# Two of the first tile's output blocks by seven products, and a new order of work around it

## The chip, the cores and the metric

One core of one Trainium2 chip. The metric is the device time of one launch in microseconds, as the median of several executions. Below, TensorE is PE in the profile (its weight loads PEld), VectorE is DVE, ScalarE is ACT, GpSimd is POOL, and SP is the engine whose queue issues nearly all DMAs.

## The reference

A recurrent attention with decay, and behind it a bilinear feed-forward layer (four sequences of 768 tokens, 8 heads of 64; model width 512, hidden width 1536):

```python
for t in range(S):
    state = gamma * state + einsum('bhd,bhde', k[t], v[t])   # per head, outer product
    y[t] = scale * einsum('bhd,bhde->bhe', q[t], state)
x = y reshaped to [3072, 512]
out = ((x @ w_a) * (x @ w_b)) @ w_out                         # float32
```

## The kernel before

The 3072 tokens are 24 slots of 128, taken in pairs. The attention of a slot is done in chunk form: k and q are scaled by powers of the decay and cast to bf16 (`scaled`, L239, mostly on POOL), k and q are transposed, `scores` (L273) gives the products of keys and queries, DVE masks them (L279), `update` (L290) adds to the state in a PSUM bank, and `inter` (L310) and `intra` (L320) give y, which ACT copies out as x, the feed-forward's input. `turn(new, old)` brings in pair `new` (state and scores) and finishes pair `old` (y's). Pairs 0 to 2 (slots 0 to 5) come by a variant with transposes on TensorE (`flip2`, L375; `update2`, L404; `inter2`, L416; `intra2`, L427); from slot 6 on the transposes are DMAs (L254).

The feed-forward works in tiles of 4, 2, 2, 2, 2, 4 and 8 slots (`TILES`). In a tile, hidden block `ft` (128 of the 1536 hidden columns) is two chains of four matmuls: `ffn_a` (L462), copied out by ACT, and `ffn_g` (L472), multiplied by it on DVE into `ht` (L474). `blocks(J, a, b)` does hidden blocks a to b of tile J. These chains rotate through three PSUM banks, the pool `psff`.

The output of a tile is by output blocks of 128 tokens. Tile 0's four are plain: `ffn_out` (L493), 12 matmuls of 512 columns each. The other tiles take two output blocks together as a 2x2 block product by seven products for eight (`Group`, with p1 to p7 of six matmuls of 256 columns, L561). They need sums of weights (`weight_sums`) and of h (`hsum`, s = 1 to 4, L503: on DVE in tile 1, on POOL in tiles 2 to 4). The products that share bank A follow one another in it: ACT takes a snapshot between them (L568), and DVE adds the snapshot to what leaves bank B or C. p6 reads sum 2, p7 sum 3, p5 sum 1, p3 sum 4. `single(J, ...)` runs tile J's group between the first three hidden blocks of tile J + 1. The last tile has its hidden blocks by seven products as well (`Unit`), with sums of w_a and w_b on POOL (`weight_pieces`).

The order on each engine is the order of the calls, written out by hand (`seq` chains the instructions of an engine in program order). A wait at the head of an engine's queue holds all that stands behind it. `casts(t)` puts on POOL slot t's k, q and (but for slots 12 to 19, whose v is cast by ACT in `v_cast`) v, and on SP's queue the transpose of slot t and behind it the loads of slot t + 2 (`load_slot`; the load of q is for two slots). The weights come in six parts of each matrix, each loaded in float32 (`load_w`, `load_o`, in the order of `LOADS`) and cast by POOL (`cast_w`, `cast_o`, L206). `warm` (L448) issues products of zeros into a bank.

Of the kernel before, what the change touches and what calls it, by code (L numbers as in the profile page):

```python
# [19 lines left out]
LOADS = "p0 p1 w0 w1 w2 w3 w4 k2 q2 a5 v2 b5 o0 o1 o2 o3 o4 o5 s6 s7".split()  # L20
# [3 lines left out]
def kernel(  # L24
# [39 lines left out]
    psff = ctx.enter_context(tc.tile_pool(name="psff", bufs=3, space=bass.MemoryType.PSUM))  # L64
    psat = ctx.enter_context(tc.tile_pool(name="psat", bufs=1, space=bass.MemoryType.PSUM))
    psst = ctx.enter_context(tc.tile_pool(name="psst", bufs=1, space=bass.MemoryType.PSUM))


# [14 lines left out]
    def load_slot(t):  # L83
        b, ci = divmod(t, NCH)
        for nm, src in (("k", k), ("q", q), ("v", v)):
# [8 lines left out]
            seq(nc.sync.dma_start(out=raws[nm, t], in_=s))  # L94

# [28 lines left out]
    def issue_loads(n):  # L124
        for _ in range(min(n, len(pending))):
            what = pending.pop(0)
            n = int(what[1:])
            if what[0] in "ab":
                load_w(n, what[0])
            elif what[0] in "kqv":  # L130
                load_two(what[0], {"k": k, "q": q, "v": v}[what[0]], 0, n, 2 * n)
            else:
                {"p": load_pair, "s": load_slot, "w": load_w, "o": load_o}[what[0]](n)
# [74 lines left out]
    def cast_w(j, names="ab"):  # L208
        sl = slice(j * WC, (j + 1) * WC)
        for nm, dst in (("a", wa_bf), ("b", wb_bf)):  # L210
            if nm in names:
                cast(nc.gpsimd, dst[:, :, sl], wst[nm, j])
# [33 lines left out]
    def casts(t):  # L246
        new_nat(t)
        scaled(nc.gpsimd, t, 0)
        scaled(nc.gpsimd, t, 1)
        if t not in range(12, 20):  # L250
            cast(nc.gpsimd, vb[t], raws["v", t])
        if t % 2 == 0:
            kqT[t // 2] = tra.tile([P, 2, 2, HP, P], BF16, tag="kqT", name="kqT", bufs=3)
        seq(nc.sync.dma_start_transpose(  # L254
            out=kqT[t // 2][:, t % 2].rearrange("p a b c -> p (a b) c"),
            in_=kqb[t].rearrange("p a hp r d -> p (a hp r d)")))
        if t + 2 < NSLOT:
            load_slot(t + 2)
# [9 lines left out]
    def scores(t, where):  # L268
        at = score_banks(where)
        for hp in range(HP):  # L270
            for c in range(2):
                for r in range(2):
                    seq(nc.tensor.matmul(at[r][half(c), hp, :],  # L273
                                         kqT[t // 2][half(r), t % 2, 0, hp, half(c)],
                                         kqT[t // 2][half(r), :, 1, hp, half(t % 2)],
                                         start=True, stop=True, skip_group_check=True))
        aT[t] = tra.tile([P, 2, HP, P], BF16, tag="aT", name="aT")
        for r in range(2):
            seq(nc.vector.tensor_tensor(aT[t][:, r], at[r], mask.to_broadcast([P, HP, P]), op=ALU.mult))  # L279

# [87 lines left out]
    def flip2(u, i, on, pool=psff, tag="ff"):  # L368
        if i == 0:
            kqT2[u] = tra.tile([P, 2, 2, HP, P], BF16, tag="kqT2", name="kqT2", bufs=2)  # L370
        for pars, eng in on:
            tp = pool.tile([P, 2, HP, P], BF16, tag=tag, name="tp")[:, : len(pars)]
            for n, par in enumerate(pars):
                for hp in range(HP):
                    seq(nc.tensor.transpose(tp[:, n, hp, :], kqb[2 * u + par][:, i, hp, :, :], ident))  # L375
            cast(eng, kqT2[u][:, pars[0] : pars[0] + len(pars), i], tp)

    def scores2(u, par, where="at"):
# [10 lines left out]
        for r in range(2):  # L389
            seq(nc.vector.tensor_tensor(aT[t][:, r], at[r], masks[par].to_broadcast([P, HP, P]),  # L390
                                        op=ALU.mult))

# [52 lines left out]
    def warm(pool, tag, *cols):  # L445
        idle = pool.tile([P, HP * P], F32, tag=tag, name="idle")
        for n in cols:
            seq(nc.tensor.matmul(idle[:, :n], zero[:, :P], zero[:, :n], start=True, stop=True,  # L448
                                 skip_group_check=True))

# [4 lines left out]
    def ffn_a(J, ft, c0=0, c1=None):  # L455
# [4 lines left out]
        a = psff.tile([P, 4 * P], F32, tag="ff", name="a")[:, : c1 - c0]  # L460
# [4 lines left out]
        seq(nc.scalar.copy(asb, a))  # L465

    def ffn_g(J, ft, c0=0, c1=None):
        c1 = TILES[J] * P if c1 is None else c1
        fs = slice(ft * P, (ft + 1) * P)
        g = psff.tile([P, 4 * P], F32, tag="ff", name="g")[:, : c1 - c0]  # L470
        for kt in range(KT):
            seq(nc.tensor.matmul(g, wb_bf[:, kt, fs], xcols(J, kt, c0, c1),  # L472
                                 start=(kt == 0), stop=(kt == KT - 1)))
        seq(nc.vector.tensor_tensor(ht[J][:, ft, c0:c1], g, asbs.pop((J, ft, c0)), op=ALU.mult))  # L474

# [12 lines left out]
    def ffn_out(J, i):  # L488
        store()
        osb = osbp.tile([P, DM], F32, tag="osb", name="osb")  # L490
        o = psff.tile([P, DM], F32, tag="ff", name="o")
        for ft in range(NFT):
            seq(nc.tensor.matmul(o, ht[J][:, ft, i * P : (i + 1) * P], wo_bf[:, ft],  # L493
                                 start=(ft == 0), stop=(ft == NFT - 1)))
        cast(nc.scalar, osb, o)
        held.append((rows(J, i // 2, i % 2), osb))
# [10 lines left out]
    def weight_sums(a, b):  # L507
        if not T1:
            T1.append(wstage.tile([P, NP, DH], BF16, tag="w", name="wsum1"))
        j = slice(a, b)  # L510
        tt(T3[:, j], B22[:, j], B12[:, j], ALU.subtract)
        tt(T2[:, j], T3[:, j], B11[:, j], ALU.add)
        tt(T4[:, j], B21[:, j], T2[:, j], ALU.subtract)
        tt(T1[0][:, j], B12[:, j], B11[:, j], ALU.subtract)

    hs = {}

    def hsum(J, s, a, b, eng=nc.vector):
        U = 2 if isinstance(J, tuple) else TILES[J] // 2
        if (J, s) not in hs:  # L520
            pool, tag = (raw, ("kf", "qf", "vf", "kf")[s - 1]) if J == (BIG, 1) else (wstage, "w")
            hs[J, s] = pool.tile([P, NP, 2, P], BF16, tag=tag, name=f"hs{s}")
        v = ht[J].rearrange("p (k j) (u r n) -> p r k j u n", k=2, r=2, n=P)
        A11, A12, A21, A22 = (v[:, r, k2, a:b, :U] for r in range(2) for k2 in range(2))
        S = {x: hs[J, x][:, a:b, :U] for x in (1, 2, 3, 4) if (J, x) in hs}
# [15 lines left out]
    class Group:  # L541

        def __init__(self, J, i, A, B, C, snaps="kqT2"):
            self.J, self.i, self.tags, self.spare = J, i, {"A": A, "B": B, "C": C}, snaps
            self.key, self.n = (J, i) if J < BIG else ((J, i // 2), i % 2)
            self.bank = {}
            self.osb = {}

        def product(self, bank, left, right, first):
            if first:  # L550
                pool, tag = self.tags[bank]
                self.bank[bank] = pool.tile([P, 4 * P], F32, tag=tag, name="m" + bank)[:, :DH]
# [33 lines left out]
        def p2(self):  # L586
            self.product("C", (0, 1), B21, True)
            tt(self.row(0)[:, :DH], self.bank["C"], self.snaps[:, 0], ALU.add)
            if self.J == BIG and self.i == 3:
# [16 lines left out]
        def p3(self):  # L606
# [8 lines left out]
            seq(nc.scalar.copy(self.row(0)[:, DH:], self.bank["A"]))  # L615
            self.leave(0)

        def p4(self):
            self.product("B", (1, 1), T4, False)
            tt(self.row(1)[:, :DH], self.bank["B"], self.snaps[:, 1], ALU.add)  # L620
            self.leave(1, 0, DH if self.J == BIG and self.i > 1 else DM)
# [57 lines left out]
    class Unit:  # L679
# [57 lines left out]
        def p3(self):  # L737
# [5 lines left out]
            else:  # L743
                tt(h_big(1)[:, self.p], self.bank["A"], half_a.pop(key), ALU.mult)

# [4 lines left out]
    def plain(w, i, c, bank):  # L750
# [10 lines left out]
        else:  # L761
            tt(h_big(c)[:, f], m, half_a.pop((i, c)), ALU.mult)

# [76 lines left out]
    ffn_a(0, 0, W2, 2 * W2)  # L840
    ffn_a(0, 1, W2, 2 * W2)
    ffn_g(0, 0, 0, W2)
# [3 lines left out]
    for ft in range(2, NFT):  # L846
# [7 lines left out]
        if ft == 7:  # L854
            scaled(D_, 4, Q)
            scaled(D_, 5, Q)
# [13 lines left out]
    ffn_g(0, 10)  # L870
# [10 lines left out]

    def v_cast(t):
        cast(nc.scalar, vb[t], raws["v", t])

    def outs(J, *rows):
        for i in rows:
            ffn_out(J, i)
# [24 lines left out]
    blocks(2, 7, 9)  # L912
    hsums(2, 0, 3, G_)
    casts(12)
    blocks(2, 9, 10)
# [20 lines left out]
    casts(16)  # L936
# [7 lines left out]
    hsum(4, 3, 0, 6, G_)  # L944
    blocks(4, 6, 8)
# [3 lines left out]
    casts(18)  # L949
# [4 lines left out]
    blocks(4, 11, NFT)  # L954
    hsums(4, 3, 6, G_)
    casts(19)
    single(4, Y0, AT0, FF)
    casts(20)
    v_cast(18)
# [3 lines left out]
    blocks(5, 5, 6)  # L963
    turn(18, 16)
# [4 lines left out]
    weight_pieces(1)  # L969
# [37 lines left out]
```

## Time and profile before

| | |
|---|---|
| median of 3 runs | 222.51 us (222.37 to 222.65) |
| the profiled execution | 222.53 us, of which the span is 220.8 us |
| PE busy in the span | 214.2 us (97%) |
| POOL busy | 140.6 us (64%) |
| DVE busy | 135.8 us (61%) |
| ACT busy | 99.2 us (45%) |

In a row of a timeline stand: start, duration, engine, line, operation, what is written and read, its shape and the number of instructions; in brackets the idle time of the engine before it and what ended that. Matmuls overlap, and the end of one is modelled: the distance of starts tells the pace. In a table of DMA issues the last number is the time from issue to landing in us.

### The profile page before, as it was taken

The numbers are of one execution on the slowest core, as the hardware profiler recorded it, in microseconds if no ns is written. First come the engines' busy times: TensorE is split into PE (matmuls) and PEld (weight loads), VectorE is DVE, ScalarE is ACT, GpSimd is POOL, SyncE is SP. The second block draws the span as 40 slices with busy tenths as digits, with TensorE's granted clock in tenths as the row PEclk, the third lists the DMA queues.
The fourth block names the chain that finished last, engine by engine and source line by source line (L and its number), as shares of the span: only waits on it lengthen the run. The fifth ranks groups of instructions, "written<-read, shape, count | busy, mean of one in ns | idle before, by whom it ended". The sixth has DMA issues, their size and how long they took to land.

```text
span 220.8 us, 5622 instructions
## 1 busy us (share of the span) xinstructions
PE 214.2 (97%) x2233; PEld 144.6 (66%) x2244; DVE 135.8 (61%) x254; ACT 99.2 (45%) x217; POOL 140.6 (64%) x155
## 2 busy tenths in 40 slices
PE   7999999999999999999999999999999999999994
PEld 3567445587458878878888665456865444448883
DVE  3785347745774473566476345776465777789642
ACT  3364333443224444354576344555536656542331
POOL 5364666777554469659846944599999999820000
PEclk9999999999999999999999999999999999999999
DMA  6999999997999999999998599990022000000055
GB/s 170 290 324 348 350 309 342 385 262 164 217 186 286 214 239 240 237 180 274 188 224 219 118 245 194 225 174 3 3 85 105 0 1 3 0 1 4 24 190 166
DMA packets 87194, 39.68 MB, mean 180 GB/s; under 512 B 57472, under 2 KB 82944, under 8 KB 87168
## 3 DMA queue, kind: packets, MB, share of 16 engines
q1 hardware_dynamic: 87024, 39.26, 76.9%
q8 instruction: 17, 0.28, 0.5%
q14 instruction: 9, 0.07, 0.1%
q10 hardware_dynamic: 144, 0.07, 0.1%
HBM read 28.31 MB, written 6.29 MB: 157 GB/s over the span
## 4 chain that ended last, share of the span: by engine, by line
PE 93%; DMA 2%; DVE 2%; issue 1%; ACT 0%; SPq 0%; DVEq 0%; ACTq 0%
PE a L462 19%; PE g L472 19%; PE mA L561 12%; PE uA L698 8%; PE mB L561 6%; PE o L493 5%; PE uB L698 4%; PE mC L561 3%; DMA qf<-in_q_dram 2%; PE at L273 2%; PE y L320 2%; PE uC L698 2%; PE st L290 2%; PE kb L756 2%; PE ka L756 2%; PE y L427 1%
## 5 line engine op out<-in xcount | busy, mean ns | idle before, releaser
L474 DVE TENSOR_TENSOR ht<-g,asb 128x256 bf16<-128x256 f32 (+1 forms) x74 | 37.1, 503 | 40.4 <-PE g L472 34.0
L472 PE MATMUL g<-xt,wb_bf 128*128 128x256 bf16 (+1 forms) x296 | 53.2, 304 | 0.4 <-DVE ht L474 0.4
L462 PE MATMUL a<-xt,wa_bf 128*128 128x256 bf16 (+1 forms) x292 | 53.4, 304 | 0.2
L465 ACT CAST asb<-a 128x256 bf16<-128x256 f32 (+1 forms) x74 | 32.2, 437 | 44.6 <-PE a L462 42.0
L472 PEld LDWEIGHTS <-wb_bf 128*128 128x128 bf16 x296 | 28.8, 98 | 13.4 <-issue 0.7
L239 POOL TENSOR_TENSOR kqb<-kf,ktab 128x512 bf16<-128x512 f32 x22 | 23.2, 1057 | 20.4 <-DMA kf<-in_k_dram 17.3
L462 PEld LDWEIGHTS <-wa_bf 128*128 128x128 bf16 x296 | 27.9, 98 | 12.2 <-issue 0.8
L561 PEld LDWEIGHTS <-hs 128*128 128x128 bf16 x240 | 23.4, 98 | 3.9
L279 DVE TENSOR_TENSOR aT<-at,mask 128x512 bf16<-128x512 f32 x36 | 22.3, 683 | 0.3
L704 ACT COPY snap<-uA 128x512 f32<-128x512 f32 x30 | 16.7, 588 | 12.6 <-PE uA L698 12.0
L239 POOL TENSOR_TENSOR kqb<-qf,qtab 128x512 bf16<-128x512 f32 x18 | 19.2, 1066 | 4.7 <-DMA qf<-in_q_dram 4.7
L503 POOL TENSOR_TENSOR hs<-ht,hs 128x384 bf16<-128x384 bf16 (+1 forms) x17 | 16.6, 982 | 5.8 <-DVE ht L474 5.8
L568 ACT COPY snaps<-mA 128x256 f32<-128x256 f32 x30 | 11.2, 373 | 19.8 <-PE mA L561 19.7
L561 PEld LDWEIGHTS <-ht 128*128 128x128 bf16 x180 | 17.5, 98 | 2.8
L503 POOL TENSOR_TENSOR hs<-ht 128x384 bf16<-128x384 bf16 (+2 forms) x12 | 13.8, 1152 | 3.7 <-DVE ht L474 3.7
L561 PE MATMUL mA<-wsum,hs 128*128 128x256 bf16 x120 | 15.7, 273 | 0.0
L206 POOL CAST vb<-vf 128x512 bf16<-128x512 f32 x16 | 10.1, 643 | 7.3 <-DMA vf<-in_v_dram 7.1
L503 POOL TENSOR_TENSOR ht<-gsb,asb 128x512 bf16<-128x512 bf16 x12 | 13.9, 1169 | 1.3 <-DVE gsb L503 1.3
L503 DVE TENSOR_TENSOR osb<-mB,snaps 128x256 f32<-128x256 f32 x20 | 8.4, 422 | 9.4 <-PE mB L561 5.1
L493 PE MATMUL o<-wo_bf,ht 128*128 128x512 bf16 x46 | 10.6, 380 | 0.1
L331 ACT CAST xt<-y 128x512 bf16<-128x512 f32 x18 | 9.7, 588 | 1.5 <-PE y L320 1.4
L448 PE MATMUL idle<-zero 128*128 128x256 f32 (+2 forms) x16 | 8.2, 632 | 1.6 <-DVE zero L140 1.5
(104 smaller groups left out, 323.0 us busy)
## 6 DMA issues: line engine op xcount, KB each, us to landing
qf<-in_q_dram SPq DMA_DIRECT2D x12, 512.0 KB, 5.7
out_dram<-osb SPq DMA_DIRECT2D x21, 256.0 KB, 3.9
kf<-in_k_dram SPq DMA_DIRECT2D x18, 256.0 KB, 4.6
vf<-in_v_dram SPq DMA_DIRECT2D x18, 256.0 KB, 5.4
wsta<-in_moe_w_a_dram SPq DMA_DIRECT2D x6, 512.0 KB, 8.4
wstb<-in_moe_w_b_dram SPq DMA_DIRECT2D x6, 512.0 KB, 8.1
wsto<-in_moe_w_out_dram SPq DMA_DIRECT2D x6, 512.0 KB, 7.6
kf<-in_k_dram SPq DMA_DIRECT2D x3, 512.0 KB, 7.1
```

The source lines that it names most:

```text
L239: seq(eng.tensor_tensor(dst, src, tab, op=ALU.mult))
L279: seq(nc.vector.tensor_tensor(aT[t][:, r], at[r], mask.to_broadcast([P, HP, P]), op=ALU.mult))
L462: seq(nc.tensor.matmul(a, wa_bf[:, kt, fs], xcols(J, kt, c0, c1), start=(kt == 0), stop=(kt == KT - 1)))
L465: seq(nc.scalar.copy(asb, a))
L472: seq(nc.tensor.matmul(g, wb_bf[:, kt, fs], xcols(J, kt, c0, c1), start=(kt == 0), stop=(kt == KT - 1)))
L474: seq(nc.vector.tensor_tensor(ht[J][:, ft, c0:c1], g, asbs.pop((J, ft, c0)), op=ALU.mult))
L493: seq(nc.tensor.matmul(o, ht[J][:, ft, i * P : (i + 1) * P], wo_bf[:, ft], start=(ft == 0), stop=(ft == NFT - 1)))
L503: seq(eng.tensor_tensor(dst, x, y, op=op))
L561: seq(nc.tensor.matmul(m, w, right[:, j], start=(first and j == 0), stop=(j == NP - 1), skip_group_check=True))
L568: seq(nc.scalar.copy(self.snaps[:, n], self.bank["A"]))
L698: seq(nc.tensor.matmul(m, w, right[:, k], start=(first and k == 0), stop=(k == 1), skip_group_check=True))
L704: seq(nc.scalar.copy(self.snaps[n], self.bank["A"]))
```

## The change

1. Tile 0: output blocks 2 and 3 go by a `Group` in place of two plain ones, spread between the halves of plain block 1 and the two turns. The sums of h that this needs (eight pieces of 128x384, on DVE) stand behind the hidden blocks 5 and 6 of tile 0 and 0 to 5 of tile 1, in buffers of the early loads. The weight sums are split into single calls. Bank reuse in `psff` is written out (class `Ring`), as some tiles are held longer.
2. The start: two of tile 0's first a's go ahead of pair 1's y's, in place of a warm-up burst, and the first two parts of each weight are cast in halves.
3. Third pair: q's scaling on DVE goes behind hidden block 8; the g's of hidden blocks 9 and 10 go ahead.
4. `casts_two(6)` casts k and q of slots 6 and 7 with their transposes ahead of both v's; loads of slots 6 to 9 go k, q, k, v, v.
5. Behind `turn(8, None)` and `turn(10, None)` three hidden blocks go as three a's, then three g's.
6. `casts` of slots 15, 16, 18 and 19 go ahead of the sums of h beside which they stood, and 8 of the last tile's 24 weight pieces go early where 1 did.

```diff
+    def casts_two(t):
+        for u in (t, t + 1):
+            new_nat(u); scaled(nc.gpsimd, u, 0); scaled(nc.gpsimd, u, 1); flip(u)
+        for u in (t, t + 1):
+            cast(nc.gpsimd, vb[u], raws["v", u])
+        load_slots(t + 2)                 # k q, k of t + 3, v, v
...
-    cast_w(0)
+    cast_w(0, parts=2)
-    warm(psff, "ff", 256)
+    ffn_a(0, 0, 0, W2)
+    ffn_a(0, 1, 0, W2)
     intra2(1, 0, True)
     inter2(1)
-    ffn_a(0, 0, 0, W2)
     intra2(1, 1, False)
     leave2(1, (A_, D_))
-    ffn_a(0, 1, 0, W2)
+    update2(1, 1)
+    ffn_g(0, 0, 0, W2)
     issue_loads(100)
-    cast_w(1)
-    update2(1, 1)
+    cast_w(1, parts=2)
...
     ffn_a(0, 9)
+    ffn_g(0, 9)
     flip2(2, Q, [((0, 1), D_)], psat, "y0")
-    ffn_g(0, 9)
+    ffn_a(0, 10)
     scores2(2, 0, "y")
     scores2(2, 1)
-    ffn_a(0, 10)
+    ffn_a(0, 11)
     update2(2, 0)
-    ffn_a(0, 11)
+    ffn_g(0, 10)
     intra2(2, 0, True)
     inter2(2)
     intra2(2, 1, False)
     leave2(2, (A_, D_))
-    ffn_g(0, 10)
     ffn_g(0, 11)
...
+    def three(J, ft):
+        store()
+        for f in range(ft, ft + 3):
+            ffn_a(J, f)
+        for f in range(ft, ft + 3):
+            ffn_g(J, f)
...
-    casts(6)
-    blocks(1, 0, 3)
-    casts(7)
-    blocks(1, 3, NFT)
-    outs(0, 0)
-    weight_sums(0, 3)
-    weight_sums(3, 6)
-    outs(0, 1)
-    casts(8)
-    outs(0, 2)
-    turn(6, None, V_)
-    hsum(1, 3, 0, 6)
-    hsums(1, 0, 6, V_)
-    outs(0, 3)
-    casts(9)
-    turn(None, 6)
+    casts_two(6)
+    for ft in range(NFT):
+        ffn_ab(1, ft)
+        if ft < 6:
+            hsum(0, (2, 1, 4)[ft // 2], ft % 2 * 3, ft % 2 * 3 + 3)
+    g = Group(0, 1, FF, FF, FF)
+    weight_sum(3)
+    weight_sum(2)
+    ffn_out(0, 0, 0)
+    ffn_out(0, 0, 1)
+    weight_sum(1, (0,))
+    casts(8)
+    g.p1()
+    g.p2()
+    weight_sum(1, (1,))
+    ffn_out(0, 1, 0)
+    turn(6, None)
+    weight_sum(4)
+    g.p7()
+    hsum(1, 3, 0, 6)
+    g.p6()
+    ffn_out(0, 1, 1)
+    g.p5()
+    casts(9)
+    turn(None, 6)
+    g.p3()
+    g.p4()
+    hsums(1, 0, 6, V_)
     single(1, AT0, AT1, FF)
...
     turn(8, None)
-    blocks(2, 7, 9)
+    three(2, 7)
...
     turn(10, None, V_)
-    blocks(3, 4, 6)
+    three(3, 4)
     hsum(3, 3, 0, 6, G_)
     v_cast(12)
-    blocks(3, 6, 8)
+    blocks(3, 7, 8)
     v_cast(13)
     blocks(3, 8, 9)
+    casts(15)
     hsums(3, 0, 3, G_)
-    casts(15)
     blocks(3, 9, 10)
     turn(12, 10)
     blocks(3, 10, NFT)
+    casts(16)
     hsums(3, 3, 6, G_)
-    casts(16)
     single(3, Y0, AT0, FF)
...
     blocks(5, 5, 6)
+    weight_pieces(6)
     turn(18, 16)
...
-    weight_pieces(1)
+    weight_pieces(2)
     turn(20, 18)
```

More of the change, by code (lines that the diff above doesn't have):

```diff
@@ L63, with __init__, tile, back @@
     osbp = ctx.enter_context(tc.tile_pool(name="osbp", bufs=6))
-    psff = ctx.enter_context(tc.tile_pool(name="psff", bufs=3, space=bass.MemoryType.PSUM))
+    ffpool = ctx.enter_context(tc.tile_pool(name="psff", bufs=1, space=bass.MemoryType.PSUM))
     psat = ctx.enter_context(tc.tile_pool(name="psat", bufs=1, space=bass.MemoryType.PSUM))
     psst = ctx.enter_context(tc.tile_pool(name="psst", bufs=1, space=bass.MemoryType.PSUM))
+    class Ring:
+        def __init__(self):
+            self.idle, self.out = ["ff0", "ff1", "ff2"], []
+        def tile(self, shape, dtype, tag, name):
+            tag = self.idle.pop(0)
+            t = ffpool.tile(shape, dtype, tag=tag, name=name)
+            self.out.append((t, tag))
+            return t
+        def back(self, *tiles):
+            for t in tiles:
+                for n, (x, tag) in enumerate(self.out):
+                    if x is t:
+                        self.idle.append(tag)
+                        del self.out[n]
+                        break
+    psff = Ring()
     last = {}
@@ L376, in flip2 @@
             cast(eng, kqT2[u][:, pars[0] : pars[0] + len(pars), i], tp)
+            psff.back(bank)
     def scores2(u, par, where="at"):
@@ L391, in scores2 @@
                                         op=ALU.mult))
+        psff.back(*at)
     def update2(u, c):
@@ L449, in warm @@
                                  skip_group_check=True))
+        psff.back(idle)
     ht = {}
@@ L459, in ffn_a @@
         fs = slice(ft * P, (ft + 1) * P)
-        a = psff.tile([P, 4 * P], F32, tag="ff", name="a")[:, : c1 - c0]
+        bank = psff.tile([P, 4 * P], F32, tag="ff", name="a")
+        a = bank[:, : c1 - c0]
         for kt in range(KT):
@@ L465, in ffn_a @@
         seq(nc.scalar.copy(asb, a))
+        psff.back(bank)
     def ffn_g(J, ft, c0=0, c1=None):
@@ L469, in ffn_g @@
         fs = slice(ft * P, (ft + 1) * P)
-        g = psff.tile([P, 4 * P], F32, tag="ff", name="g")[:, : c1 - c0]
+        bank = psff.tile([P, 4 * P], F32, tag="ff", name="g")
+        g = bank[:, : c1 - c0]
         for kt in range(KT):
@@ L474, in ffn_g @@
         seq(nc.vector.tensor_tensor(ht[J][:, ft, c0:c1], g, asbs.pop((J, ft, c0)), op=ALU.mult))
+        psff.back(bank)
     def ffn_ab(J, ft):
@@ L486, in store, with ffn_out @@
         held.clear()
[L488 to L496, printed above, removed]
+    plain_out = {}
+    def ffn_out(J, i, n):
+        if n == 0:
+            store()
+            plain_out[i] = psff.tile([P, DM], F32, tag="ff", name="o")
+        o = plain_out[i]
+        for ft in range(NP * n, NP * n + NP):
+            seq(nc.tensor.matmul(o, ht[J][:, ft, i * P : (i + 1) * P], wo_bf[:, ft],
+                                 start=(ft == 0), stop=(ft == NFT - 1), skip_group_check=True))
+        if n:
+            osb = osbp.tile([P, DM], F32, tag="osb", name="osb")
+            cast(nc.scalar, osb, o)
+            psff.back(o)
+            held.append((rows(J, i // 2, i % 2), osb))
     def rows(J, u, r):
@@ L545, in __init__ @@
             self.key, self.n = (J, i) if J < BIG else ((J, i // 2), i % 2)
-            self.bank = {}
+            self.bank, self.whole = {}, {}
             self.osb = {}
@@ L551, in product @@
                 pool, tag = self.tags[bank]
-                self.bank[bank] = pool.tile([P, 4 * P], F32, tag=tag, name="m" + bank)[:, :DH]
+                self.whole[bank] = pool.tile([P, 4 * P], F32, tag=tag, name="m" + bank)
+                self.bank[bank] = self.whole[bank][:, :DH]
             m, J = self.bank[bank], self.key
@@ L588, in p2 @@
             tt(self.row(0)[:, :DH], self.bank["C"], self.snaps[:, 0], ALU.add)
+            psff.back(self.whole["C"])
             if self.J == BIG and self.i == 3:
@@ L615, in p3 @@
             seq(nc.scalar.copy(self.row(0)[:, DH:], self.bank["A"]))
+            psff.back(self.whole["A"])
             self.leave(0)
@@ L620, in p4 @@
             tt(self.row(1)[:, :DH], self.bank["B"], self.snaps[:, 1], ALU.add)
+            psff.back(self.whole["B"])
             self.leave(1, 0, DH if self.J == BIG and self.i > 1 else DM)
@@ L744, in p3 @@
                 tt(h_big(1)[:, self.p], self.bank["A"], half_a.pop(key), ALU.mult)
+            psff.back(self.bank["A"])
         def p4(self):
@@ L944 @@
     hsum(4, 3, 0, 6, G_)
+    casts(18)
     blocks(4, 6, 8)
```

89 lines of the change are left out of this document (54 added, 35 removed).

## The prediction

> **What bounds the kernel now.** First the page's busy shares, the clock and the chain that ended last.
>
> ```profile
> span 220.8 us, 5622 instructions
> PE 214.2 (97%) x2233; PEld 144.6 (66%) x2244; DVE 135.8 (61%) x254; ACT 99.2 (45%) x217; POOL 140.6 (64%) x155
> PEclk9999999999999999999999999999999999999999
> PE 93%; DMA 2%; DVE 2%; issue 1%; ACT 0%; SPq 0%; DVEq 0%; ACTq 0%
> ```
>
> TensorE at full clock is the path. A gain must shorten its work or close a gap in it, and stays only if no later place makes TensorE wait for something that has not moved. So I read the timeline of each engine around every edited line. The profiled execution took 222.53 us with a span of 220.8, so 1.7 us lie around the span; the median of the runs is 222.51, and I sum against 222.53.
>
> TensorE's cadence, from the distance between starts (the second column holds the pipelined end):
>
> ```profile
> 53.73 7.93 PE L493 MATMUL o<-wo_bf,ht 128*128 128x512 bf16 x35
> 61.59 0.32 PE L290 MATMUL st<-vb,kqb 128*64 128x64 bf16 x8
> 72.17 0.82 PE L561 MATMUL mA<-wo_bf,hs 128*128 128x256 bf16 x6
> 72.83 0.82 PE L561 MATMUL mB<-wsum,ht 128*128 128x256 bf16 x6
> 66.27 0.83 PE L561 MATMUL mA<-wo_bf,ht 128*128 128x256 bf16 x6
> ```
>
> Three output blocks are 36 matmuls (one record is missing) in 7.86 us less a small change-over: 0.216 us for a 512-column matmul. Six 256-column ones take 0.66 us: 0.109 each. The last row is the first product of tile 1, a mark for later.
>
> **First blocks sooner.** One warm-up burst goes and two a's move up behind it, on half casts.
>
> ```profile
> 15.70 0.70 PE L448 MATMUL idle<-zero 128*128 128x256 f32 x2
> 18.49 1.04 POOL L206 CAST wb_bf<-wstb 128x1024 bf16<-128x1024 f32 x1 [1.91 <-DMA wstb<-in_moe_w_b_dram]
> 22.08 1.03 PE L462 MATMUL a<-xt,wa_bf 128*128 128x512 bf16 x4
> 14.04 1.17 POOL L206 CAST vb<-vf 128x512 bf16<-128x512 f32 x2 [1.46 <-DMA vf<-in_v_dram]
> ```
>
> Half a cast is a 128x512 one, 0.58 us (1.17 for two). The first g then starts at about 18.49 + 0.58 + 0.1 = 19.15 and five further half blocks of 0.44 bring block 2 to 21.8, against 22.08: 0.3 us early. Two halves cost 1.17 against 1.04; the four pairs hide in POOL's waits for DMA like the 1.91 us one, and without that cover would cost 0.13 each. But the gain cannot pass the third pair:
>
> ```profile
> 32.45 2.04 POOL L239 TENSOR_TENSOR kqb<-kf,ktab 128x512 bf16<-128x512 f32 x2 [0.76 <-DMA kf<-in_k_dram]
> 34.17 0.77 PE L375 MATMUL tp<-ident,kqb 128*128 128x128 bf16 x8
> 34.78 1.03 PE L462 MATMUL a<-xt,wa_bf 128*128 128x512 bf16 x4
> 38.96 1.04 POOL L206 CAST wb_bf<-wstb 128x1024 bf16<-128x1024 f32 x1 [0.26 <-DMA wstb<-in_moe_w_b_dram]
> 40.12 0.42 PE L427 MATMUL y<-aT,vb 64*64 64x128 bf16 x16
> 43.11 0.60 PE L462 MATMUL a<-xt,wa_bf 128*128 128x256 bf16 x4
> ```
>
> The second k of that pair is scaled at 34.49, after a load that POOL already waited for. TensorE comes to these transposes at 33.9 and still leaves them at 34.78. I count 0 (a gain of 0.3 if the load came earlier; a loss only if the start slips by over 0.45).
>
> **Third pair's order.** Block 10's g moves ahead of the pair's products. It needs the last weight cast, which waited for DMA and ends at 40.0. What then has to follow, that g, the y's and the last g, is what stood between 40.12 and 43.11: 2.99 us, so 43.1 again. DVE's q scaling, now behind block 8's eviction, no longer delays it, but the later wait covers that. 0, with 0.15 either way.
>
> **Seven products for eight.** Two output blocks, 24 x 0.216 = 5.19 us, become 42 x 0.109 = 4.59: **0.60 us less on the path**. The products' snapshots on ACT and sums on DVE lie beside another output block's halves, or a turn and a product. The sums of h are eight new DVE pieces of 128x384. The six in tile 1's blocks stand beside POOL's casts:
>
> ```profile
> 54.03 0.61 POOL L206 CAST vb<-vf 128x512 bf16<-128x512 f32 x1
> 54.34 0.71 DVE L503 TENSOR_TENSOR wsum<-wo_bf 128x768 bf16<-128x768 bf16 x1
> 55.09 0.56 DVE L503 TENSOR_TENSOR wsum<-wsum,wo_bf 128x768 bf16<-128x768 bf16 x1
> 157.53 0.69 DVE L503 TENSOR_TENSOR xs<-xt 128x1024 bf16<-128x1024 bf16 x1 [3.79 <-ACT xt L331]
> 159.22 1.15 DVE L503 TENSOR_TENSOR xs<-xt 128x1024 bf16<-128x1024 bf16 x1
> 53.13 0.42 DVE L474 TENSOR_TENSOR ht<-g,asb 128x256 bf16<-128x256 f32 x1 [0.45 <-PE g L472]
> ```
>
> Beside a cast a sum took 0.71 against 0.56, and where POOL's own sums ran without a break 1.15 against 0.69: 0.15 to 0.46 more. Alone, 384 columns are some 0.35 us (estimated from 0.56 for 768). DVE is idle 0.45 us in each block of 0.87, so 0.35 + 0.15 is 0.05 over, 0.3 in six blocks. With three banks, g's bank is wanted again two half blocks (0.87) after g, and the eviction takes 0.42, so it may lag by about 0.4. I take 0, from the row with a cast, since POOL's neighbours there are casts; by the other row it is (0.42 + 0.81 - 0.87) x 6 - 0.4 = 1.7 us of stall. The Trainium skill ("SBUF — State Buffer", "Who interferes with whom") says that a DVE instruction with two SBUF inputs and a GpSimd one that reads SBUF exclude each other for a whole instruction. The 0.71 row is shorter than that rule gives, for the cast ends 0.3 us after that sum begins; by the rule TensorE would stall in tile 1.
>
> **a's ahead of g's.** Behind the two turns that only bring in a pair, DVE is busy with four masked products:
>
> ```profile
> 78.19 0.61 PE L462 MATMUL a<-xt,wa_bf 128*128 128x256 bf16 x4
> 81.17 0.42 PE L310 MATMUL y<-kqT,gst 64*64 64x128 bf16 x16
> 92.91 0.61 PE L462 MATMUL a<-xt,wa_bf 128*128 128x256 bf16 x4
> 95.80 0.60 PE L472 MATMUL g<-xt,wb_bf 128*128 128x256 bf16 x4 [0.35 <-DVE ht L474]
> 98.95 0.32 PE L290 MATMUL st<-vb,kqb 128*64 128x64 bf16 x8
> 95.33 0.75 DVE L474 TENSOR_TENSOR ht<-g,asb 128x256 bf16<-128x256 f32 x2
> ```
>
> Tile 2: three blocks (6 x 0.437 = 2.62) took 2.98; 0.08 is the change-over that stays: **0.28 gained**. Tile 3: six blocks (5.24) took 6.04, less 0.09: 0.71. But with three a's first, the fourth needs the first g's bank, free only when DVE leaves the masked products and has evicted it: 95.33 + 0.38 + 0.1 = 95.81, against 92.91 + 2.62 = 95.53, both before the shift. A new wait of 0.28, and **0.43 gained**. Sum so far 0.60 + 0.28 + 0.43 = 1.31.
>
> **POOL's new order at tile 3 takes some back.** The casts of slots 15 and 16 go ahead of the sums of h, and slot 16's cast now stands between a load and the product p6 (sum 2):
>
> ```profile
> 81.07 0.91 POOL L503 TENSOR_TENSOR hs<-ht,hs 128x384 bf16<-128x384 bf16 x1 [1.86 <-DVE ht L474]
> 93.46 1.04 POOL L239 TENSOR_TENSOR kqb<-qf,qtab 128x512 bf16<-128x512 f32 x1 [1.46 <-DMA qf<-in_q_dram]
> 94.53 2.94 SPq L254 DMA_TRANSPOSE kqT<-kqb  x1
> 98.14 0.58 SPq L99 DMA_DIRECT2D qf<-in_q_dram  x1
> 103.43 0.91 POOL L503 TENSOR_TENSOR hs<-ht,hs 128x384 bf16<-128x384 bf16 x1
> 105.36 0.82 PE L561 MATMUL mA<-wsum,hs 128*128 128x256 bf16 x6
> qf<-in_q_dram SPq DMA_DIRECT2D x1, 512.0 KB, 5.7
> qf<-in_q_dram SPq DMA_DIRECT2D x1, 512.0 KB, 5.0
> 103.54 1.29 SPq L254 DMA_TRANSPOSE kqT<-kqb  x1
> ```
>
> Before, that sum's second half was done at 104.3, a microsecond ahead of p6. Now it follows a chain: tile 2's sums start when block 8's g is evicted (0.60 earlier, less 0.13 as three() puts that g later, so 0.47 earlier), slot 12's cast follows, then slot 14's load, cast and transpose, then slot 16's load, all moved by 0.47. The q load issues at 97.67. The two load rows are that load itself (5.7) and the next pair's (5.0); I take 5.5, nearer its own. So it lands at 103.17, the cast runs to 104.2, the half sum 0.9 to 105.1, and p6's fourth matmul (the first three need the first half) starts then. Without the wait it would come at 105.36 - 1.31 + 0.33 = 104.38. Stall 0.72, by the ends of the load 0.2 to 0.9. Queued behind p6 is TensorE's whole program.
>
> The other moves cost nothing that I can find. At tile 4 slot 18's cast fills a POOL wait. The six weight pieces moved up in tile 5 fill POOL's waits for loads, and POOL is not on the path there. In SP's queue the first loads go k, q, k, v, v, so slot 7's transpose issues sooner, as its turn comes sooner. Sum: -1.31 + 0.72 = -0.59, so 222.53 - 0.59 = **221.9**.
>
> **Rivals.** (1) The chain at tile 3 does not bind: a transpose's issue took 2.94 us there but 1.29 elsewhere, which alone brings q 1.65 us sooner. Then all of 1.31 stays: 221.2. Against it: the long one has a pair of loads in front, as it will have again. (2) Slower: in tile 1's blocks DVE's sums wait for POOL's casts, g's evictions fall behind, and TensorE waits for a bank. It costs nothing below 0.52 us for a sum (0.87 - 0.42 + 0.4/6), and turns the total into a loss from about 0.62 us on (a stall of 0.6). At 0.81 us, 1.7 us of stall: tile 2's evictions, and the chain behind them, come that much later, so 221.9 + 1.7 = 223.6. For it the 1.15 row, against it the 0.71 row. (3) The seven products do not save: the waits between snapshot and next product take the 0.60 back. Then the chain is 0.6 later too: 222.5. Against it, tile 1's own seven products run at 0.109 without a gap.
>
> **How the numbers follow.** Forecast 0.52 (221.6 to 222.3 by the load's ends and the 0.15 above), rival 1 0.18, rival 2 0.17, rival 3 0.13. A change of 0.2%, 0.45 us, is about what a measurement here can tell. Faster by more: rival 1 and seven tenths of the forecast, 0.54. Within: the rest of the forecast and half of rival 3, 0.22. Slower: rival 2, half of rival 3, 0.24 with rounding. The range 220.9 to 223.0 takes in rival 1 with the early 0.3, rival 3, and small stalls of rival 2; the full 223.6 stays out.
>
> **What would show it.** In the profile after: the third pair's transposes still end near 34.8 and tile 1 starts near 43.1; single(1) starts 0.6 us earlier than 66.27; no gap among tile 1's blocks, and DVE's 128x384 sums below 0.5 us; tile 2's and 3's bursts without the 0.35 us wait for DVE; POOL's q cast of slot 16 waits for DMA, and p6 of tile 3 has a gap of some 0.7 us in it. A gap before 66, or p6 without one, makes the forecast wrong.

## The result and the profile after

The changed kernel is **slower: 231.72 us** (median of 5 runs, 231.4 to 232.37) against 222.43 us (5 runs, 222.1 to 222.65); the ratio is 1.042, with a 95% interval of 1.041 to 1.043. The forecast was 221.9, its range ended at 223.0, and its dearest rival stood at 223.6. The profiled execution took 231.4 us with a span of 229.7, against 222.53 and 220.8.

From the page of the changed kernel: the span, the busy times, the rows of slices of PE and of its clock, and the chain by engine.

```profile
span 229.7 us, 5681 instructions
PE 214.9 (94%) x2260; PEld 146.5 (64%) x2260; DVE 144.1 (63%) x264; ACT 99.9 (43%) x220; POOL 141.9 (62%) x159
PE   7899999905999999999999999999999999999994
PEclk9999999995999999999999999999999999999999
PE 77%; DMA 12%; SPq 5%; POOL 3%; DVE 1%; issue 1%; ACT 0%; DVEq 0%
```

TensorE's busy time hardly moved (214.2 to 214.9), but the share fell from 97 to 94%. The row of slices says where: one slice of 5.7 us in which TensorE does nothing, between 46 and 52 us, and after it one in which its clock is at half. The chain, which was 93% TensorE, is 77% TensorE now, and most of the rest goes through DMA, SP's queue and POOL.

The timeline of TensorE at that place (start, duration, and in brackets the idle time before and what ended it), then DVE's and POOL's:

```profile
45.47 0.60 PE L521 MATMUL g<-xt,wb_bf 128*128 128x256 bf16 x4
54.20 1.01 PE L509 MATMUL a<-xt,wa_bf 128*128 128x256 bf16 x4 [8.12 <-DVE ht L523]
55.00 1.06 PE L521 MATMUL g<-xt,wb_bf 128*128 128x256 bf16 x4
58.21 0.60 PE L521 MATMUL g<-xt,wb_bf 128*128 128x256 bf16 x4
63.88 2.75 PE L546 MATMUL o<-wo_bf,ht 128*128 128x512 bf16 x12
```

```profile
44.33 0.42 DVE L523 TENSOR_TENSOR ht<-g,asb 128x256 bf16<-128x256 f32 x1 [0.21 <-PE g L521]
53.08 0.73 DVE L559 TENSOR_TENSOR hs<-ht,hs 128x384 bf16<-128x384 bf16 x1 [8.33 <-POOL kqb L267]
53.73 0.41 DVE L523 TENSOR_TENSOR ht<-g,asb 128x256 bf16<-128x256 f32 x1
```

```profile
49.95 1.04 POOL L267 TENSOR_TENSOR kqb<-qf,qtab 128x512 bf16<-128x512 f32 x1 [0.59 <-DMA qf<-in_q_dram]
52.00 1.04 POOL L267 TENSOR_TENSOR kqb<-qf,qtab 128x512 bf16<-128x512 f32 x1
```

Read from right to left, the last bracket first. TensorE stops after block 2 of tile 1: the three banks go round, the a of block 3 needs the one with the g of block 1, and DVE has not evicted that g. DVE has not because at the head of its queue, right behind block 0's eviction, stands the first piece of sum 2 of tile 0 (`hs`, L559), which waits 8.33 us for an instruction of POOL that has nothing to do with sums: the scaling of q. The two POOL rows are the casts of q of slots 6 and 7; the second ends at 53.04, and 0.04 us later DVE goes on. In the built kernel sum 2 lies at byte 105664 of each partition, and so does the float32 q of slots 6 and 7, which came by one load. The tag that the sum takes its buffer from has three buffers, and the one it got was still to be read by POOL. Sum 1 (97472) and sum 3 (126144) got buffers whose readers were long done.

The clock in three stretches around it (length, then for each engine busy time and number of instructions, PEclk, DMA share, GB/s):

```profile
49.00:54.20 5.20, 0.00 (x1) 0.00 (x1) 1.12 (x3) 0.00 (x0) 4.59 (x6) 0.71 0.81 167
54.20:56.00 1.80, 1.80 (x9) 1.27 (x9) 0.89 (x3) 0.37 (x1) 0.08 (x1) 0.50 0.91 161
58.30:60.00 1.70, 1.70 (x18) 1.52 (x17) 1.35 (x4) 0.74 (x2) 1.04 (x1) 1.00 1.25 262
```

TensorE comes back at half clock, so its next half blocks take 0.80 to 0.86 us instead of 0.437 until about 58.0. That costs another 2.0 us: tile 1's blocks end at 63.88 against 53.73, 10.15 later, of which 8.12 are the stop.

The remaining steps can be read off how far TensorE lags behind the kernel before at marks in the program (start of the mark in the timelines; the last two columns are experiments described below):

| mark | before, us | changed, lag | own buffer, lag | all three mended, lag |
|---|---|---|---|---|
| end of tile 1's blocks | 53.73 | +10.15 | +1.49 | +0.04 |
| `single(1)`, p1 | 66.27 | +9.46 | +1.57 | -0.66 |
| `single(2)`, p1 | 83.92 | +9.19 | +1.39 | -0.92 |
| key-query products of `turn(12, 10)` | 99.19 | +8.76 | +0.96 | -1.36 |
| `single(3)`, p1 | 102.52 | +8.75 | +0.95 | -1.36 |
| key-query products of `turn(14, 12)` | 112.68 | +8.85 | +2.79 | -1.36 |
| last p3 | 216.75 | +8.84 | +2.79 | -0.72 |

The gains that the forecast counted are all in the lag column of the changed kernel: 0.69 at the seven products (from the first mark to the second), 0.27 and 0.43 at the two bursts (three a's ahead of three g's).

### The profile page after: what moved, and what is told of

Its sections match the earlier page's. It is cut to its first block, busy times and chain, and to the rows that moved or that the text cites. A ratio compares the mean times of both kernels' runs of the same rounds, so it can differ in the third digit from the quotient of the medians.

```text
span 229.7 us, 5681 instructions
## 1 busy us (share of the span) xinstructions
PE 214.9 (94%) x2260; PEld 146.5 (64%) x2260; DVE 144.1 (63%) x264; ACT 99.9 (43%) x220; POOL 141.9 (62%) x159
## 4 chain that ended last, share of the span: by engine, by line
PE 77%; DMA 12%; SPq 5%; POOL 3%; DVE 1%; issue 1%; ACT 0%; DVEq 0%
PE a L509 15%; PE g L521 14%; PE mA L625 13%; PE uA L765 8%; PE mB L625 6%; DMA wstb<-in_moe_w_b_dram 4%; DMA kf<-in_k_dram 4%; PE uB L765 4%; DMA qf<-in_q_dram 4%; SPq L126 3%; PE mC L625 3%; PE at L314 2%; PE o L546 2%; POOL kqb L267 2%; PE y L362 2%; PE uC L765 2%
## 5 line engine op out<-in xcount | busy, mean ns | idle before, releaser
L509 PE MATMUL a<-xt,wa_bf 128*128 128x256 bf16 (+1 forms) x296 | 54.1, 309 | 8.3 <-DVE ht L523 8.1
L521 PE MATMUL g<-xt,wb_bf 128*128 128x256 bf16 (+1 forms) x296 | 53.8, 308 | 0.1
L625 PEld LDWEIGHTS <-hs 128*128 128x128 bf16 x264 | 25.5, 98 | 4.7 <-POOL hs L559 0.2
L632 ACT COPY snaps<-mA 128x256 f32<-128x256 f32 x33 | 12.3, 373 | 22.0 <-PE mA L625 21.8
L559 POOL TENSOR_TENSOR hs<-ht 128x384 bf16<-128x384 bf16 (+2 forms) x12 | 13.8, 1152 | 12.7 <-DVE ht L523 12.7
L625 PEld LDWEIGHTS <-ht 128*128 128x128 bf16 x198 | 19.4, 98 | 3.2
L559 POOL TENSOR_TENSOR hs<-ht,hs 128x384 bf16<-128x384 bf16 (+1 forms) x17 | 16.7, 981 | 4.2 <-DVE ht L523 4.1
L559 POOL TENSOR_TENSOR ht<-gsb,asb 128x512 bf16<-128x512 bf16 x12 | 13.6, 1158 | 6.7 <-DVE gsb L559 6.7
L625 PE MATMUL mA<-wsum,hs 128*128 128x256 bf16 x132 | 17.5, 273 | 0.0
L233 POOL CAST vb<-vf 128x512 bf16<-128x512 f32 x16 | 10.9, 693 | 8.4 <-DMA vf<-in_v_dram 8.1
L559 DVE TENSOR_TENSOR osb<-mB,snaps 128x256 f32<-128x256 f32 x22 | 9.2, 423 | 10.8 <-PE mB L625 6.5
L559 DVE TENSOR_TENSOR hs<-ht,hs 128x384 bf16<-128x384 bf16 (+3 forms) x11 | 8.2, 742 | 8.4 <-POOL kqb L267 8.3
L559 DVE TENSOR_TENSOR hs<-ht 128x384 bf16<-128x384 bf16 (+3 forms) x13 | 9.9, 758 | 0.0
```

What stands on the lines that cost most here:

```text
L233: seq(engine.tensor_copy(dst, src))
L509: seq(nc.tensor.matmul(a, wa_bf[:, kt, fs], xcols(J, kt, c0, c1), start=(kt == 0), stop=(kt == KT - 1)))
L559: seq(eng.tensor_tensor(dst, x, y, op=op))
L625: seq(nc.tensor.matmul(m, w, right[:, j], start=(first and j == 0), stop=(j == NP - 1), skip_group_check=True))
L632: seq(nc.scalar.copy(self.snaps[:, n], self.bank["A"]))
```

## The experiments

All times are medians; each ratio is to the kernel before on the same chip, with its 95% interval. "F" is the changed kernel with the own buffer of the first experiment.

**A buffer of its own.**

```diff
+    own = ctx.enter_context(tc.tile_pool(name="own", bufs=1))
...
+            if (J, s) == (0, 2):
+                hs[J, s] = own.tile([P, NP, 1, P], BF16, tag="hs", name="hs2own")
+                return
...
```

> Sum 2 of tile 0 gets a buffer of its own (1536 bytes of each partition that nothing else uses), all else as in the changed kernel. Theory (shared buffer: sum 2 is written where q of slots 6 and 7 lies until POOL has cast it): the stop of 8.1 us in tile 1's blocks is gone, DVE's sum stands right behind block 0's eviction, the time is 221.0 to 222.3 us, near the forecast. Rival (a two-input sum of DVE cannot run beside POOL's casts): the stop stays, about 231.7 us.

Measured: 224.61 us, ratio 1.009 (1.007 to 1.011). The stop of 8.1 us is gone and with it the half clock, and 7.1 us of the 9.3. So the shared buffer is the main cause. But 2.1 us of loss remain where the theory expected none. In this kernel's timelines of TensorE, DVE and POOL:

```profile
47.29 0.60 PE L510 MATMUL a<-xt,wa_bf 128*128 128x256 bf16 x4 [0.34 <-DVE ht L524]
48.73 0.60 PE L510 MATMUL a<-xt,wa_bf 128*128 128x256 bf16 x4 [0.41 <-DVE ht L524]
49.98 0.60 PE L510 MATMUL a<-xt,wa_bf 128*128 128x256 bf16 x4 [0.22 <-DVE ht L524]
67.19 0.82 PE L630 MATMUL mB<-wsum,ht 128*128 128x256 bf16 x6 [0.61 <-DVE osb L560]
108.47 0.50 PE L630 MATMUL mA<-wsum,hs 128*128 128x256 bf16 x3 [1.67 <-POOL hs L560]
```

```profile
44.66 0.88 DVE L560 TENSOR_TENSOR hs2own<-ht,hs 128x384 bf16<-128x384 bf16 x1
45.79 1.12 DVE L560 TENSOR_TENSOR hs2own<-ht,hs 128x384 bf16<-128x384 bf16 x1
47.16 1.19 DVE L560 TENSOR_TENSOR hs<-ht 128x384 bf16<-128x384 bf16 x1
48.27 0.41 DVE L524 TENSOR_TENSOR ht<-g,asb 128x256 bf16<-128x256 f32 x1
48.61 0.99 DVE L560 TENSOR_TENSOR hs<-ht 128x384 bf16<-128x384 bf16 x1
49.86 0.34 DVE L560 TENSOR_TENSOR hs<-ht,hs2own 128x384 bf16<-128x384 bf16 x1
50.46 0.86 DVE L560 TENSOR_TENSOR hs<-ht,hs2own 128x384 bf16<-128x384 bf16 x1
```

```profile
44.28 1.04 POOL L234 CAST wo_bf<-wsto 128x1024 bf16<-128x1024 f32 x1 [0.31 <-DMA wsto<-in_moe_w_out_dram]
45.66 1.04 POOL L234 CAST wo_bf<-wsto 128x1024 bf16<-128x1024 f32 x1 [0.33 <-DMA wsto<-in_moe_w_out_dram]
47.10 1.04 POOL L234 CAST wo_bf<-wsto 128x1024 bf16<-128x1024 f32 x1 [0.40 <-DMA wsto<-in_moe_w_out_dram]
48.34 1.04 POOL L268 TENSOR_TENSOR kqb<-kf,ktab 128x512 bf16<-128x512 f32 x1 [0.20 <-PE g L522]
50.06 1.04 POOL L268 TENSOR_TENSOR kqb<-qf,qtab 128x512 bf16<-128x512 f32 x1 [0.68 <-DMA qf<-in_q_dram]
```

Put the two lists side by side. The five long sums end at 45.54, 46.91, 48.35, 49.60 and 51.32; POOL's instructions end at 45.32, 46.70, 48.14, 49.38 and 51.10. Each sum ends 0.21 or 0.22 us after POOL's instruction, however long it has been standing there. The sum at 49.86 begins in a pause of POOL and takes 0.34. A sum with two inputs in SBUF is not slowed by POOL, it waits until POOL's instruction is over. The evictions, with one input from PSUM, take 0.41 or 0.42 in all of this. The Trainium skill ("SBUF — State Buffer", "Who interferes with whom") states just that, an exclusive lock held for the whole instruction, and by these rows the trace agrees with it. The mean sum takes 0.90 us, and blocks 4 to 6 start 1.43 us late in all (0.50, 0.56 and 0.37, from the distances of the starts). Of the last two rows of TensorE the first, 0.61 us ahead of p4, is a relative of this second cause: p4's bank is emptied by DVE behind a two-input sum. The other, 1.67 us inside p6 of tile 3, is a third cause, taken up below.

**The same buffer, two blocks later.**

```diff
-("kf", "qf", "vf", "kf")[s - 1]
+(("qf", "kf", "vf", "kf") if J == 0 else ("kf", "qf", "vf", "kf"))[s - 1]
```

> Only the tags of sums 1 and 2 of tile 0 are exchanged: sum 1, first written two blocks later than sum 2, now lies on the q of slots 6 and 7, sum 2 on pair 2's k. Theory: DVE waits for the same end of POOL's q cast (about 53.0 us), but reaches the wait two blocks (1.75 us) later, so the stop stands ahead of block 5 and is 8.1 - 1.75 = 6.4 us; time about 230.0 us. Rival (port): the first sum behind block 0 waits as before, 231.7 us.

Measured: 230.89 us, ratio 1.037 (1.035 to 1.039). From its timeline of TensorE:

```profile
54.28 1.01 PE L509 MATMUL a<-xt,wa_bf 128*128 128x256 bf16 x4 [5.92 <-DVE ht L523]
```

**The same sums, six blocks later.**

```diff
-        if ft < 6:
-            hsum(0, (2, 1, 4)[ft // 2], ft % 2 * 3, ft % 2 * 3 + 3)
+        if ft >= 6:
+            hsum(0, (2, 1, 4)[ft // 2 - 3], ft % 2 * 3, ft % 2 * 3 + 3)
```

> The same sums in the same buffers, each six blocks later (behind blocks 6 to 11). Theory: the wait ends at the same instant and is reached 6 x 0.874 = 5.2 us later, so the stop is 8.1 - 5.2 = 2.9 us ahead of block 9, time 226.5 us, or down to 224.7 if so short a stop keeps TensorE's clock. Rival (port): sums run only once POOL's whole run of casts is over (54.3 us), a stop of over 4 us, or none if they may run between two casts.

Measured: 226.44 us, ratio 1.018 (1.015 to 1.021).

```profile
54.24 1.01 PE L509 MATMUL a<-xt,wa_bf 128*128 128x256 bf16 x4 [2.96 <-DVE ht L523]
```

From the changed kernel over the exchanged tags to this one the stop begins later each time and ends at the same instant, 54.20, 54.28, 54.24: 8.12, 5.92 and 2.96 us, where 6.4 and 2.9 were expected of the last two. (With the exchanged tags the two sums that now come first also stood beside casts, and 0.5 us more of stop came ahead of the long one, in two pieces.) So the end is set by POOL's cast, not by DVE or by what the sums compute. The clock fell to half in this profiled execution as well (granted clock 0.50 from 55 to 57 us), so a stop of 2.96 us was enough here. It is not always: of the six executions five have a mean granted clock of 0.992, and the sixth 0.999 and the shortest time, 225.70 us.

**TensorE kept at work in the stop.**

```diff
     for ft in range(NFT):
+        if ft == 3:
+            warm(psat, "y1", *[512] * 8)
```

> As the changed kernel, with eight products of zeros into a spare bank ahead of tile 1's block 3, where TensorE stops. Theory of the clock: the stop stays 8 us, but TensorE is kept at work in it, the five half blocks after it take 0.437 instead of 0.855 us, and the time falls by 1 to 2 us, to about 230 us. Rival (the slow half blocks come of DVE catching up with evictions): they stay at 0.855 and the time at 231.7 us.

Measured: 230.87 us, ratio 1.036 (1.034 to 1.038), 0.85 us less than the changed kernel. Its timeline of TensorE:

```profile
45.93 7.03 PE L493 MATMUL idle<-zero 128*128 128x512 f32 x16
54.37 0.60 PE L509 MATMUL a<-xt,wa_bf 128*128 128x256 bf16 x4 [1.41 <-DVE ht L523]
54.80 0.60 PE L521 MATMUL g<-xt,wb_bf 128*128 128x256 bf16 x4
```

The stop is as long, but the half blocks behind it keep 0.437 us. Tile 1's blocks end at 62.23, 1.65 us earlier than in the changed kernel; 1.36 are left at the last p3. So the slow stretch is the clock, not DVE catching up. The Trainium skill ("TensorE: Matmul & The Clock Gate", Part 1) gives an idle window of about 3.4 us for the fall to half clock, and about as long a stretch of work for the return. The traces agree in part. After the stops of 8.12, 5.92 and 2.96 us the slow work lasted 3.8, 5.6 and 3.2 us, near its figure twice and well above it once. The granted clock fell 5.1, 4.7 and 2.75 us after TensorE had gone idle, the last one shorter than its figure. So the length of the stop alone does not tell here when the clock falls and returns.

**The old order of POOL at tile 3**, in F: the casts of slots 15 and 16 again behind the sums of h.

```diff
-    casts(15)
     hsums(3, 0, 3, G_)
+    casts(15)
...
-    casts(16)
     hsums(3, 3, 6, G_)
+    casts(16)
```

> Sum 2 of tile 0 in a buffer of its own, and at tile 3 the casts of slots 15 and 16 again behind the sums of h, as in the kernel before. The run with only the own buffer stopped 1.67 us in p6 of tile 3. Theory (the cast of slot 16, waiting for its load, stands between the eviction and sum 2): the stop goes, 1.5 to 1.8 us less than with the own buffer alone, about 222.9 us. Rival (POOL is late there anyway, from the 1.4 us that tile 1 lost): the stop stays or moves into tile 4, 224.2 to 224.6.

Measured: 223.84 us, ratio 1.005 (1.004 to 1.006). In F, POOL's rows ahead of p6's second half (108.47, above) were the cast of slot 16's q and then the half sum:

```profile
106.50 1.04 POOL L268 TENSOR_TENSOR kqb<-qf,qtab 128x512 bf16<-128x512 f32 x1 [1.00 <-DMA qf<-in_q_dram]
107.50 0.91 POOL L560 TENSOR_TENSOR hs<-ht,hs 128x384 bf16<-128x384 bf16 x1
```

With the old order p6 of tile 3 has no stop any more, and the last p3 starts at 217.84 against 219.54 in F. In time it is only 0.8 us less, since the executions of F scatter from 224.1 to 225.4 and the profiled one was the slowest.

**Sums behind every second block**, in F.

```diff
-        if ft < 6:
-            hsum(0, (2, 1, 4)[ft // 2], ft % 2 * 3, ft % 2 * 3 + 3)
+        if ft % 2 == 0:
+            hsum(0, (2, 1, 4)[ft // 4], ft // 2 % 2 * 3, ft // 2 % 2 * 3 + 3)
```

> Own buffer, the changed order at tile 3 kept, and the six pieces of tile 0's sums behind every second block of tile 1 (0, 2, ... 10) instead of behind blocks 0 to 5. Theory (each sum ends only with POOL's running cast and so takes some 0.9 us; one to a block of 0.874 us beside a 0.41 us eviction is too much, one to two blocks, 0.9 + 2 x 0.41 = 1.72 of 1.75, is not): single sums still take 0.8 to 1.2 us, but the three stops of 1.4 us in blocks 3 to 5 go. As POOL and the loads behind p6 of tile 3 are not earlier for that, part comes back there: 223.3 to 224.3 us. Rival (the stops come of something else, the number of sums or banks): blocks 3 to 5 stop as before, 224.6.

Measured: 223.42 us, ratio 1.003 (1.001 to 1.006), its executions between 222.2 and 225.5. One stop of 0.28 us is left of the three ahead of blocks 4 to 6 (the expectation counts them as blocks 3 to 5), and it now stands ahead of block 9. Sums took from 0.35 to 1.19 us, by whether a cast was running. The stop in p6 of tile 3 became 1.15 us.

**All three mended**: own buffer, sums behind every second block, the old order at tile 3.

> Own buffer, sums behind every second block, and the old order at tile 3 together. Theory: with all three causes taken away what is left is the gain that was forecast for the seven products and the a's ahead of g's, less what DVE's longer sums still cost: 221.2 to 221.9 us. Rival (the gains were never there, or are lost at a later wait): 222.3 us or more.

Measured: **221.81 us, ratio 0.996 (0.994 to 0.997)**, faster than the kernel before. Tile 1's blocks run without a stop, and the steps in the last column of the table are the forecast's gains: 0.70 from the seven products, 0.26 and 0.44 from the bursts. Of the lead of 1.36, 0.64 are lost later: in this execution 0.30 in a wait for a DMA transpose at `turn(16, 14)` and 0.32 in a wait for DVE at tile 5.

**The bursts undone**, in the kernel with all three mended.

```diff
-    three(2, 7)
+    blocks(2, 7, 10)
...
-    three(3, 4)
+    blocks(3, 4, 7)
```

> The same as the run with all three causes taken away, with tile 2's and tile 3's blocks behind the turns again one by one instead of three a's ahead of three g's. Theory: tile 2's blocks take 0.28 us more and tile 3's 0.43 us more, 0.7 us in all. Rival: the wait for DVE only moves on, no difference within 0.2 us.

Measured: 223.04 us, ratio 1.002 (1.001 to 1.003), 1.2 us more. From the key-query products of the turn that only brings in a pair to the next mark of the table, tile 2 takes 7.04 us against 6.35 and tile 3 7.29 against 6.42: more than the kernel before took (6.60 and 6.85). The a's ahead of the g's are worth what was forecast against the kernel before, and more against this one; why more was not followed up. Its profiled execution also lost 0.8 us up to `single(1)`, ahead of the edit.

**Sums on POOL instead of DVE**, buffers shared as in the changed kernel, old order at tile 3.

```diff
-            hsum(0, (2, 1, 4)[ft // 2], ft % 2 * 3, ft % 2 * 3 + 3)
+            hsum(0, (2, 1, 4)[ft // 2], ft % 2 * 3, ft % 2 * 3 + 3, G_)
```

> As the changed kernel, buffers shared as there, with the six pieces of sums 2, 1 and 4 of tile 0 on POOL instead of DVE, where they stand behind its casts of slots 6 and 7, and with the old order at tile 3. Theory (what stopped TensorE was DVE, held up ahead of g's evictions, by the buffer first and by POOL's running casts second): tile 1's blocks run without a stop although POOL's casts and the buffers are as before; 221.3 to 222.2 us, the upper end if DVE's weight sums, now beside POOL's sums, hold up a product. Rival (the buffer's wait itself delays the products p6 and p5): a stop of a microsecond or more about 62 us, 223 us or more.

Measured: 223.54 us, ratio 1.004 (1.003 to 1.006). Tile 1's blocks end at 53.79 without a stop: the same wait for the buffer costs nothing in POOL's queue, where the cast stands ahead anyway. But the loss came back one step on, as neither theory said in size:

```profile
54.40 2.36 DVE L559 TENSOR_TENSOR wsum<-wo_bf 128x768 bf16<-128x768 bf16 x2
56.68 2.45 DVE L559 TENSOR_TENSOR wsum<-wsum,wo_bf 128x768 bf16<-128x768 bf16 x2
```

```profile
60.71 0.81 PE L625 MATMUL mB<-wsum,hs 128*128 128x256 bf16 x6 [0.51 <-DVE osb L559]
67.39 0.81 PE L625 MATMUL mB<-wsum,ht 128*128 128x256 bf16 x6 [1.70 <-DVE osb L559]
```

DVE's weight sums now run beside POOL's sums; two take 2.4 us instead of 1.02, POOL's pieces up to 1.2 instead of 0.91. DVE comes late to the additions that empty the products' banks, and p7 and p4 wait 2.2 us. p6 and p5 start without a stop, so the rival did not occur, though the time lies where it would. The conflict went along with the work.

**Only slot 15's cast early**, in the kernel with all three mended.

```diff
+    casts(15)
     hsums(3, 0, 3, G_)
-    casts(15)
```

> The run with all three causes taken away, with slot 15's cast ahead of tile 3's sums of h again, as in the change, and slot 16's behind them. Theory (slot 16's cast, waiting for its load, is what makes p6 of tile 3 wait): no stop, or under 0.3 us, in p6, 221.7 to 222.0 us. Rival (either cast ahead of the sums is enough, by 2 us of POOL's time): a stop of 0.7 us or more, 222.4 us or more.

Measured: 221.37 us, ratio 0.995 (0.994 to 0.997). p6 of tile 3 has no stop. So slot 15's cast ahead of the sums is not enough: the stop needs slot 16's, with its wait for a load. Slot 16's cast ahead alone was not run.

**The start as before**, in the kernel with all three mended (warm-up burst, whole casts, a's between the second pair's products).

> The run with all three causes taken away, with the first blocks as in the kernel before (warm-up burst, whole casts, a's between the second pair's products). Theory: the 0.3 us gained there are lost again at the third pair's transposes, no difference within 0.2 us. Rival: 0.3 us slower.

Measured: 223.56 us, ratio 1.005 (1.003 to 1.007): 1.75 us slower than with the new start, where a difference within 0.2 was expected. DVE's timeline in the two, the old start first:

```profile
35.27 2.12 DVE L268 TENSOR_TENSOR kqb<-qf,qtab 128x512 bf16<-128x512 f32 x2
```

```profile
34.81 1.28 DVE L268 TENSOR_TENSOR kqb<-qf,qtab 128x512 bf16<-128x512 f32 x2
```

TensorE does leave the third pair's K transposes at nearly the same time (34.84 against 34.72). But DVE's scaling of q begins 0.46 us later, runs into a cast of POOL (35.62 to 36.84), takes 2.12 for 1.28, and q's transposes wait 0.50 us; tile 1 starts at 43.67 for 43.13. The rest of the loss is at the same sums and casts as in F (0.19 at block 11, 0.94 at p4). That they meet differently because the start shifts is argued, not tested.

**The third pair's order as before**, in the kernel with all three mended.

> The run with all three causes taken away, with the third pair's products in the order of the kernel before. Theory: 0, with 0.15 us either way, tile 1 starting near 43.1 us. Rival: DVE's scaling of q, again ahead of block 8's eviction and now behind tile 0's first sums, is late, 0.3 to 0.8 us slower.

Measured: 221.46 us, ratio 0.995 (0.994 to 0.997). No difference that these executions can tell (221.1 to 221.8 here, 221.1 to 222.0 with the new order), tile 1 at 43.06.

## Why the prediction was wrong

**The step that failed** is in the seven products: "The sums of h are eight new DVE pieces ... I take 0". It failed twice.

First, it asked how long a sum takes and beside what it runs, but not whose buffer it writes. That term is missing altogether, and it is the whole main cause: 8.1 us of stop and 2.0 us of half clock. The forecast knew that the sums lay in buffers of the early loads, but did not go through which load, and who still had to read it. Of the three buffers of early loads that the sums took, one belonged to slots 6 and 7, whose casts stand late on POOL in that stretch. The question that step should have put for each new write, behind which read must it stand, would have led to POOL's queue, and from there to the evictions queued behind the sum on DVE. The sum did not start a wait of its own; it put an old one of POOL's at the head of DVE's queue. This is why the mark "a gap before 66" in the forecast caught it, though no rival had the cause.

Second, the price of a sum beside a cast. The step took 0.15 us from the row of 0.71 against 0.56, as though POOL slowed DVE by a share. That row's sum began at 54.34 beside a cast that ended at 54.64, so it met only the last 0.3 us of the cast, and it ended 0.41 us after it. The kernel before has another weight sum beside POOL, which the forecast did not show:

```profile
57.30 1.36 POOL L239 TENSOR_TENSOR kqb<-kf,ktab 128x512 bf16<-128x512 f32 x1 [2.66 <-DMA kf<-in_k_dram]
57.80 1.28 DVE L503 TENSOR_TENSOR wsum<-wo_bf,wsum 128x768 bf16<-128x768 bf16 x1
```

It took 1.28 us for 0.56 and ended 0.42 us after POOL's instruction: again a wait for its end, and no share. The rule of the Trainium skill that spoke against the change was named there and set aside by the 0.71 row; the traces bore the rule out. **Rival 2** had this place, this mechanism and this threshold (a loss from 0.62 us a sum; 1.7 us of stop at 0.81). Measured with the buffer out of the way: 0.90 us a sum, 1.43 us late in the blocks, and again 0.61 at p4; 224.61 us against its 223.6. It had 0.17 of the chance and should have had most of it.

**The chain behind p6 of tile 3** was right in place and mechanism and mis-sized: 0.72, 0.2 to 0.9, was forecast. With the own buffer p6's fourth matmul starts 1.83 us late (1.67 as idle time), with the sums spread 1.31. The mis-sized term is mostly the load of slot 16's q, taken as 5.5 us: it took 6.4 and 6.0 from issue to landing. In the changed kernel itself it cost 0.10, presumably because POOL and the loads ran on while TensorE stood still. That slot 16's cast makes the chain was right.

**Seven products** were worth 0.69 in the changed kernel against 0.60, **the bursts** 0.27 and 0.43 against 0.28 and 0.43. Block 2 began at 21.78 (21.8 forecast), tile 1 at 43.17 (43.1). **Third pair's order**: 0, as forecast. **First blocks sooner**: the 0.3 us are lost at the K transposes, as forecast, but in this kernel the step is not worth 0. Undone beside the new order of the third pair it costs 0.54 us at tile 1's start, because of DVE's q scaling and not of TensorE. Rival 1 (p6 does not wait) held in the changed kernel, presumably only because of the stop; rival 3 did not occur. With all three causes mended the time, 221.81, is about the one forecast, but this is more chance than the forecast's sum: there the p6 stall was taken away, and two other waits took as much back.

That the scatter of F and of the spread sums (over 1 us, against 0.7 for the kernel before) comes from where sums and casts meet is only argued, from sums that took 0.35 in one execution and 1.17 in another at the same place.

## What to carry to other kernels

When a step is added that writes a buffer from a shared tag, find out which buffer it gets and which instruction reads that one last; a write at the head of an in-order queue waits for that reader, and all evictions behind it wait too. Cost two-input work of DVE beside a busy POOL by POOL's whole remaining instruction, and place it in POOL's pauses or so sparsely that evictions catch up. A stop of a few us on TensorE can cost more than itself, as the clock may fall and has to come back.

## What the runs showed of the hardware that was not expected

The wait of a two-input DVE sum for POOL is exact: the sum ended 0.21 to 0.22 us after POOL's instruction in five of five cases, and took 0.34 us where it began in a pause of POOL. It works the other way as well: POOL's pieces beside DVE's weight sums took up to 1.2 us for 0.91. TensorE's clock was at half after a stop of only 2.96 us, by the mean clocks in five of six executions; products of zeros for 7.0 of the 8.4 us of a stop kept it at full.
